# A fused attention and MoE kernel: input fetched earlier, batches interleaved, activation table loaded ahead, token sums as an extra matmul column

## The chip, the cores and the metric

The kernel runs on one core of a Trainium2 chip. The metric is the device time of one execution in microseconds (us). It includes about 2 us around the span that the profile shows, from the first to the last instruction: the profiled run of the kernel before took 255.27 us and its span is 253.5 us. PE is TensorE, PEld its weight loads, DVE is VectorE, ACT ScalarE, POOL GpSimd, SP SyncE.

## The reference

Eight batches go through a small cross attention between 512 tokens and 32 state rows for each of 8 heads, in both directions. Its result, 544 rows a batch, goes through a two-layer network with SiLU.

```python
scores = scale * x @ state.T            # (B,H,512,32)
a  = softmax(scores);   xread = a @ state       # 512 rows of 64 per head
a2 = softmax(scores.T); sread = a2 @ x          # 32 rows of 64 per head
x_moe = concat([xread, sread]) -> (8*544, 512)
out = silu(x_moe @ w_in) @ w_out                # d_ff = 2048
```

The kernel folds the state into the first weight: `W1 = state_blockdiag @ w_in`, so that `G1 = silu(W1.T @ aT)` needs only the normalised attention weights `aT`, and `G2 = G1.T @ w_out`. The sread rows are few and are done for all batches at the end (called batch 8).

## The kernel before

A batch passes through these steps, and each name is a helper that the schedule calls. The kernel keeps eight PSUM banks (the buffers that matmuls write), named o0, o1, w0, w1, h0, h1, a0 and a1; in the cuts below AB and HB stand for the pairs a0/a1 and h0/h1, and DA and DD for the two engines that copy a pair out (VectorE and ScalarE, or VectorE twice). aT is the normalised attention weights, transposed.

```python
def g1(b, ft):     # 2 matmuls of 512 columns, then SiLU on ScalarE
    ...
    nc.scalar.activation(g[b % 2][:, ft, :], bk[:], func=SILU, bias=0.0)
def g2(b, tt, ft, bk): ...      # 1 matmul of 512 columns, accumulated over 16 ft
def w1_m / w1_e                 # W1 = state x w_in, 8 small matmuls; copies out of PSUM
def cast_x, x_T, sc, ex         # x to bf16, transposes, scores, exponentials (EXP table)
def norm_s, norm_m, a_T         # row sums and reciprocal, multiply, transposes of the weights
def sread_m(b, bk):
    v = bank[bk]
    for half in range(2):
        for c in range(4):
            for kt in range(KT):
                nc.tensor.matmul(v[ds(32 * kt, 32), ds(D * half, D)],
                    en[b % 2][:, c, half, kt, :], x_n[b % 2][:, kt, c, half, :], ...)
    for half in range(2):               # the sums over tokens: a column of ones
        for c in range(4):
            nc.tensor.matmul(v[:, ds(128 + half, 1)],
                en[b % 2][:, c, half, :, :], ones[:], ...)
```

The schedule is written by hand. All weights are requested first, in chunks of 512 KB on the POOL queue; x of batch 1 is requested in the middle of batch 0. From batch 2 on it runs in phases: phase k does the G2 of batch k and, woven into it, the attention and G1 of batch k+1.

```python
load_w(0); load_st(1)
for j in range(1, 4): load_w(j)
...
sread_t(0, "a1", "dve")
W1x(0, 1, AB, DA)
gate(1)                      # makes the load of x wait until here
load_x(1, nc.sync)
cast_x(1, "dve", (0, 1)); cast_x(1, "pool", (2, 3))
...
for k in range(2, 7):
    n = k + 1
    ex(n, 0, 2, "a0"); ex(n, 2, 2, "a1")          # loads the EXP table
    W1p(n, 0); norm_s(n); norm_m(n, "pool")
    add(fill, 18, W1p(n, 1), sread_m(n, "a1"), sread_n(n, "a1"))
    add(fill, 29, a_T(n, (("a0", "act"),)))
    for i in range(16):
        add(fill, 32 + 1.9 * i, g1(n, i))          # the first one loads the SiLU table
    phase(k, fill)                                 # 64 G2, with the fill between them
```

The softmax here doesn't subtract the row's maximum and nothing guards it: scores larger than these inputs give would overflow.

## Time and profile before

| | kernel before |
|---|---|
| median | 256.44 us (3 runs, 254.75 to 257.2) |
| span, mean granted clock | 253.5 us, 0.980 |
| PE / ACT / DVE / POOL busy | 90% / 50% / 38% / 17% |

The first view is the windows view of the kernel before: for each stretch of time its length and each engine's busy time, with the number of instructions. PEclk is the granted clock of TensorE as a share of full speed; the last two columns are the DMA engines' busy share (in this view it exceeds 1 at times) and what they moved.

```profile
...
core 0: us, PE busy (x) PEld busy (x) DVE busy (x) ACT busy (x) POOL busy (x), PEclk, DMA share, GB/s
12.08:14.48 2.40, 1.81 (x17) 0.99 (x18) 1.17 (x3) 1.19 (x2) 1.05 (x2) 0.50 1.33 199
14.48:31.00 16.52, 15.97 (x111) 6.08 (x111) 2.02 (x7) 7.66 (x14) 3.17 (x5) 0.88 1.23 219
31.00:34.50 3.50, 0.00 (x0) 0.00 (x0) 0.95 (x3) 0.38 (x1) 0.98 (x3) 1.00 0.96 118
34.50:54.80 20.30, 16.72 (x127) 7.71 (x127) 9.12 (x18) 9.85 (x15) 2.53 (x3) 0.92 0.18 56
...
118.50:144.80 26.30, 24.89 (x218) 12.02 (x218) 11.60 (x22) 14.16 (x23) 4.74 (x9) 1.00 0.26 80
...
```

From 118.5 us on PE is busy for 24.89 of 26.3 us: these phases are bound by TensorE. Before 54.8 us it is different: from 14.48 us PE is busy for 15.97 of 16.52 us, but at a mean clock of 0.88; in the third row it does nothing at all for 3.5 us, and in the fourth it is busy for 16.72 of 20.3 us.

The second view is the timeline of PE in the kernel before. Columns: start, duration, engine, source line, operation, out<-in and the number of instructions merged; in brackets the idle time before and what ended it.

```profile
...
12.08 1.03 PE L181 MATMUL ps_a<-ident,an 128*128 128x128 bf16 x8 [1.66 <-DVE an L165]
...
14.48 2.74 PE L255 MATMUL ps_h<-aT,W 128*128 128x512 bf16 x6 [0.59 <-DVE W L79]
...
18.72 0.42 PE L191 MATMUL ps_a<-x_n,en 128*32 128x64 bf16 x32
19.07 0.35 PE L202 MATMUL ps_a<-ones,en 128*128 128x1 bf16 x8
19.29 0.59 PE L255 MATMUL ps_h<-aT,W 128*128 128x512 bf16 x2
...
29.66 1.03 PE L255 MATMUL ps_h<-aT,W 128*128 128x512 bf16 x4
34.52 0.40 PE L128 MATMUL ps_a<-ident,x_n 128*128 128x128 bf16 x4 [3.83 <-DVE x_n L79]
...
42.16 0.90 PE L234 MATMUL ps_a<-w_in_sb,sbd 64*32 64x512 bf16 x8 [1.73 <-ACT en L150]
...
```

The line of 34.52 us shows the hole: the transposes of x of batch 1 wait for DVE's cast, which waits for the DMA. The lines of 18.72 and 19.07 us show the sread group: 32 matmuls of 64 columns take 0.35 us from start to start of the next, and the eight matmuls of one column after them take 0.22 us.

The third view is the timeline of all engines in phase 3, around its first G1.

```profile
...
127.37 1.02 ACT L83 ACTIVATE aT<-ps_a 128x1024 bf16<-128x1024 bf16 x1 [6.44 <-PE ps_a L181]
...
128.44 0.59 PE L255 MATMUL ps_h<-aT,W 128*128 128x512 bf16 x2 [0.47 <-ACT aT L83]
...
129.12 1.28 ACT L263 ACT_TABLE_LOAD   x1 [0.72 <-PE ps_h L255]
...
129.52 0.59 PE L279 MATMUL ps_o<-w_out_sb,g 128*128 128x512 bf16 x2
...
130.41 1.09 ACT L263 ACTIVATE g<-ps_h 128x512 bf16<-128x512 f32 x2
131.06 0.59 PE L255 MATMUL ps_h<-aT,W 128*128 128x512 bf16 x2 [0.94 <-ACT g L263]
...
```

The first G1 waits for the copy of aT on ACT (128.44 us). Then ACT loads the SiLU table (129.12 us, 1.28 us) before it can drain that G1, and the third G1 has no free bank until 131.06 us.

### The profile page before, as it was taken

The numbers are of one execution on the slowest core, as the hardware profiler recorded it, in microseconds if no ns is written. First come the engines' busy times: TensorE is split into PE (matmuls) and PEld (weight loads), VectorE is DVE, ScalarE is ACT, GpSimd is POOL, SyncE is SP. The second block draws the span as 40 slices with busy tenths as digits, with TensorE's granted clock in tenths as the row PEclk, the third lists the DMA queues.
The fourth block names the chain that finished last, engine by engine and source line by source line (L and its number), as shares of the span: only waits on it lengthen the run. The fifth ranks groups of instructions, "written<-read, shape, count | busy, mean of one in ns | idle before, by whom it ended". The sixth has DMA issues, their size and how long they took to land.

```text
span 253.5 us, 4473 instructions
## 1 busy us (share of the span) xinstructions
PE 226.9 (90%) x1832; PEld 112.4 (44%) x1832; DVE 95.8 (38%) x187; ACT 126.4 (50%) x201; POOL 43.8 (17%) x81
## 2 busy tenths in 40 slices
PE   5699846899978999799979997999799988999994
PEld 4534223335334544354435443544354444466653
DVE  3722032482671447132914192409330850011110
ACT  3644516456816670757075726563466437733300
POOL 4732020322070005200340034002400110000000
PEclk9959989999999999999999999999999999999999
DMA  6999930086001116110810081017201120111112
GB/s 178 169 202 206 251 39 0 0 276 224 4 36 47 44 49 202 43 41 21 230 41 30 14 243 51 0 44 208 86 0 41 44 83 3 41 43 41 59 68 84
DMA packets 19829, 22.08 MB, mean 87 GB/s; under 512 B 3040, under 2 KB 15584, under 8 KB 19808
## 3 DMA queue, kind: packets, MB, share of 16 engines
q1 hardware_dynamic: 12576, 16.39, 19.8%
q0 software_dynamic: 6128, 4.42, 11.7%
q10 hardware_dynamic: 1104, 0.98, 1.1%
q8 instruction: 14, 0.23, 0.3%
q14 instruction: 7, 0.06, 0.1%
HBM read 17.30 MB, written 8.91 MB: 103 GB/s over the span
## 4 chain that ended last, share of the span: by engine, by line
PE 77%; ACT 7%; DVE 6%; DMA 6%; issue 3%; ACTq 0%; DVEq 0%
PE ps_o L279 39%; PE ps_h L255 21%; DMA x_f<-in_x_dram 6%; PE ps_h L266 3%; PE ps_a L128 3%; ACT aT L83 2%; PE ps_w L279 2%; PE ps_w L234 2%; ACT g L263 2%; PE ps_a L181 2%; DVE W L79 2%; DVE rs L160 2%; PE ps_a L139 1%; ACT L263 1%; DVE x_n L79 1%
## 5 line engine op out<-in xcount | busy, mean ns | idle before, releaser
L279 PE MATMUL ps_o<-w_out_sb,g 128*128 128x512 bf16 x480 | 133.4, 381 | 1.1 <-DVE o_sb L79 1.0
L263 ACT ACTIVATE g<-ps_h 128x512 bf16<-128x512 f32 x128 | 75.4, 597 | 48.0 <-PE ps_h L255 47.2
L255 PE MATMUL ps_h<-aT,W 128*128 128x512 bf16 x256 | 76.8, 385 | 9.5 <-ACT g L263 4.7
L279 PEld LDWEIGHTS <-g 128*128 128x128 bf16 x512 | 47.8, 98 | 53.6 <-issue 6.6
L79 DVE COPY o_sb<-ps_o 128x512 f32<-128x512 f32 x30 | 20.3, 684 | 65.4 <-PE ps_o L279 65.4
L255 PEld LDWEIGHTS <-W 128*128 128x128 bf16 x256 | 24.8, 99 | 40.2 <-issue 12.9
L165 POOL TENSOR_TENSOR an<-en,rs 128x1024 bf16<-128x1024 bf16 x7 | 13.4, 1913 | 124.0 <-DVE rs L161 112.3
L83 ACT ACTIVATE aT<-ps_a 128x1024 bf16<-128x1024 bf16 (+1 forms) x8 | 7.3, 918 | 37.8 <-PE ps_a L181 37.8
L81 POOL CAST x_n<-x_f 128x256 bf16<-128x256 f32 x52 | 18.5, 405 | 22.4 <-DMA x_f<-in_x_dram 22.4
L79 DVE CAST W<-ps_w 128x512 bf16<-128x512 f32 x29 | 18.7, 684 | 7.8 <-PE ps_w L234 7.8
L128 PEld LDWEIGHTS <-x_n 128*128 128x128 bf16 x128 | 9.2, 106 | 8.5 <-DVE x_n L79 5.8
L79 DVE CAST W<-ps_h 128x512 bf16<-128x512 f32 x20 | 12.8, 681 | 0.0
L160 DVE TENSOR_REDUCE rs<-en 128x32 f32<-128x1024 bf16 (+1 forms) x11 | 10.2, 923 | 6.9 <-ACT en L150 6.9
L128 PE MATMUL ps_a<-ident,x_n 128*128 128x128 bf16 x112 | 8.9, 225 | 4.2 <-DVE x_n L79 4.2
L79 DVE COPY sbd<-ps_a 64x128 bf16<-64x128 bf16 x14 | 4.0, 288 | 21.9 <-PE ps_a L117 21.8
L79 DVE COPY xT<-ps_a 128x1024 bf16<-128x1024 bf16 x13 | 8.9, 691 | 8.8 <-PE ps_a L128 4.9
L274 ACT ACTIVATE g_s<-ps_h 128x256 bf16<-128x256 f32 x16 | 6.2, 384 | 11.6 <-PE ps_h L266 11.6
L263 ACT ACT_TABLE_LOAD x7 | 9.0, 1283 | 3.7 <-PE ps_h L255 3.6
L279 PE MATMUL ps_w<-w_out_sb,g 128*128 128x512 bf16 x32 | 10.3, 406 | 0.0
L266 PE MATMUL ps_h<-xsT,w_in_sb 128*128 128x256 bf16 x64 | 9.6, 273 | 0.0
L79 DVE CAST x_n<-x_f 128x256 bf16<-128x256 f32 x12 | 3.9, 383 | 13.9 <-DMA x_f<-in_x_dram 13.9
L150 ACT ACT_TABLE_LOAD x7 | 9.0, 1283 | 0.1
(60 smaller groups left out, 139.8 us busy)
## 6 DMA issues: line engine op xcount, KB each, us to landing
out_dram<-o_sb SPq DMA_DIRECT2D x32, 256.0 KB, 2.4
x_f<-in_x_dram SPq DMA_DIRECT2D x7, 1024.0 KB, 6.7
w_in_sb<-in_moe_w_in_dram POOLq DMA_DIRECT2D x4, 512.0 KB, 11.6
w_out_sb<-in_moe_w_out_dram POOLq DMA_DIRECT2D x4, 512.0 KB, 13.9
x_f<-in_x_dram SPq DMA_DIRECT2D x2, 256.0 KB, 3.0
x_f<-in_x_dram ACTq DMA_DIRECT2D x2, 256.0 KB, 3.8
out_dram<-o_sb ACTq DMA_DIRECT2D x1, 256.0 KB, 2.5
st_nat<-in_state_dram POOLq DMA_DIRECT2D x7, 32.0 KB, 14.2
```

Of the source, the lines that this page charges most:

```text
L79: nc.vector.tensor_copy(dst, src)
L81: nc.gpsimd.tensor_copy(dst, src)
L83: nc.scalar.activation(dst, src, func=COPY, bias=0.0)
L128: nc.tensor.transpose(v[:, kt % 2, c, :], x_n[b % 2][:, kt, c, :, :], ident[:])
L150: nc.scalar.activation(en[b % 2][:, :, :, ds(kt, n), :].rearrange("p c h k s -> p k (c h) s"), v[:, ds(kt % 2, n)], func=EXP, bias=0.0, sc ...
L160: nc.vector.tensor_reduce(v, en[b % 2][:, :, :, ds(kt, n), :], axis=AX, op=ADD)
L165: e.tensor_tensor(an[b % 2][:, :, :, ds(kt, n), :].rearrange("p c h k s -> p (c h) k s"), en[b % 2][:, :, :, ds(kt, n), :].rearrange("p c ...
L255: nc.tensor.matmul(bk[:], W1[b % 2][:, half, ds(128 * ft, 128)], aT[b % 2][:, half, :, :], start=(half == 0), stop=(half == 1), skip_group ...
L263: nc.scalar.activation(g[b % 2][:, ft, :], bk[:], func=SILU, bias=0.0)
L266: nc.tensor.matmul(bk[:, 0:256], w_in_sb[:, kt, ds(128 * ft, 128)], xsT[:, kt, :, :, :], start=(kt == 0), stop=(kt == KT - 1), skip_group_ ...
L274: nc.scalar.activation(g_s[:, ft, :], bk[:, 0:256], func=SILU, bias=0.0)
L279: nc.tensor.matmul(bank[bk][:, c0:c1], src[:, ft, ds(128 * tt, 128)], w_out_sb[:, ft, c0:c1], start=(ft == 0), stop=(ft == 15), skip_group ...
```

## The change

The change has three intents: to fill the hole at the start by fetching x of batch 1 right behind the first weight chunks and by interleaving G1 of batch 1 with batch 0; to take small matmuls away from PE; and to take two waits out of each phase. Its core, with cuts marked:

```diff
-    ones = pers.tile([128, 1], BF16, name="ones")
-    x_n = [pers.tile([128, KT, 4, 2, D], BF16, ...
+    x_n = [pers.tile([128, KT, 4, 132], BF16, ...      # columns 1 and 130 hold ones
 ...  sread_m: 65 columns instead of 64, the group with ones[:] removed
-                        v[ds(32 * kt, 32), ds(D * half, D)],
+                        v[ds(32 * kt, 32), ds((D + 1) * half, D + 1)],
-                        x_n[b % 2][:, kt, c, half, :],
+                        x_n[b % 2][:, kt, c, ds(1 + (D + 1) * half, D + 1)],
 ...  start
-        load_w(0)
+        load_wi(0); load_wo(0)
         load_st(1)
-        for j in range(1, 4):
-            load_w(j)
+        load_x(1, nc.gpsimd, 0, 2)
+        load_x(1, nc.gpsimd, 2, 2)
 ...  the other weights follow later; W1 of batch 0 before its a_T; normalisation in
 ...  halves instead of quarters, shared with POOL
+        for ft in range(4):
+            g1(0, ft)
+        G2(0, 0) ... G2(0, 3), between them cast_x(1), xTs(1), scs(1)
+        exs(1); norm_s(1); norm_m(1, "dve")
+        W1x(0, 1, AB, DA)
+        W1x(1, 0, HB, DA)
+        nc.scalar.preload_act_table(SILU)
+        a_T(1, (("a0", "dve"),))
+        g1(0, 4) ... g1(0, 7), G2(0, 4), g1(1, 0), G2(0, 5), g1(1, 1), ...   # to g1(1, 10)
 ...  phases
-                w1_e(b, 2 * i + j, WP[j], ("dve", "dve"))
+                w1_e(b, 2 * i + j, WP[j], DD if j == 0 else ("act", "act"))
+            add(fill, s, L(nc.scalar.preload_act_table, SILU))     # after the exponentials and the first W1 copies
-            add(fill, 29, L(a_T, n, (("a0", "act"),)))
+            add(fill, a0, L(a_T, b, (("a0", "act"),)))             # a0 = 24
-                add(fill, 32 + 1.9 * i, L(g1, n, i))
+                add(fill, sg + dg * i, L(g1, b, i))                # 28 + 2.15 * i
```

Batch 1 becomes a phase of the same form, with its last five G1 at the start.

More of the change, by code (lines that the diff above doesn't have):

```diff
@@ L47 @@
     x_f = [pers.tile([128, KT, 2, 256], FP32, name=f"x_f{i}") for i in range(2)]
-    x_n = [pers.tile([128, KT, 4, 2, D], BF16, name=f"x_n{i}") for i in range(2)]
+    x_n = [pers.tile([128, KT, 4, 132], BF16, name=f"x_n{i}") for i in range(2)]
     xT = [pers.tile([128, KT, 4, 128], BF16, name=f"xT{i}") for i in range(2)]
@@ L94, in gate, with load_wi @@
         nc.vector.memset(x_f[b % 2][ds(0, 1), 0, 0, ds(0, 1)], 0.0)
-    def load_w(j):
+    def load_wi(j):
         nc.gpsimd.dma_start(
@@ L99, in load_w, with load_wo @@
         )
+    def load_wo(j):
         nc.gpsimd.dma_start(w_out_sb[:, ds(4 * j, 4), :], wout_re[:, ds(4 * j, 4), :])
@@ L110, in cast_x @@
                     eng,
-                    x_n[b % 2][:, kt, :, h, :],
+                    x_n[b % 2][:, kt, :, ds(2 + D * h, D)],
                     x_f[b % 2][:, kt, h, :].rearrange("p (c d) -> p c d", c=4),
@@ L128, in x_T @@
             nc.tensor.transpose(
-                v[:, kt % 2, c, :], x_n[b % 2][:, kt, c, :, :], ident[:]
+                v[:, kt % 2, c, :], x_n[b % 2][:, kt, c, ds(2, 128)], ident[:]
             )
@@ L199, in sread_m @@
                     )
-        for half in range(2):
-            for c in range(4):
-                nc.tensor.matmul(
-                    v[:, ds(128 + half, 1)],
-                    en[b % 2][:, c, half, :, :],
-                    ones[:],
-                    start=(c == 0),
-                    stop=(c == 3),
-                    skip_group_check=True,
-                )
     def sread_n(b, bk):
         v = bank[bk]
-        nc.vector.reciprocal(srec[:], v[:, 128:130])
+        nc.vector.reciprocal(srec[:], v[:, 0:130:129])
         nc.vector.tensor_tensor(
             sr[:],
-            v[:, 0:128].rearrange("p (h d) -> p h d", h=2),
+            v[:, 1:129].rearrange("p (h d) -> p h d", h=2),
             srec[:].unsqueeze(2).to_broadcast([128, 2, D]),
@@ L311 @@
         nc.scalar.dma_start(st0_f[:], state[0].rearrange("h ns d -> ns h d"))
-        load_x(0, nc.sync, 0, 1)
-        load_x(0, nc.scalar, 1, 1)
-        load_x(0, nc.sync, 2, 1)
-        load_x(0, nc.scalar, 3, 1)
+        for kt in range(KT):
+            load_x(0, nc.sync, kt, 1)
         nc.vector.memset(zeros[:], 0.0)
         nc.vector.memset(sbd[:], 0.0)
-        nc.vector.memset(ones[:], 1.0)
+        for i in range(2):
+            nc.vector.memset(x_n[i][:, :, :, 1:131:129], 1.0)
         make_identity(nc, ident[:])
@@ L321 @@
         cp("pool", st_nat[:, 0, :], st0_f[:])
-        load_w(0)
+        load_wi(0)
+        load_wo(0)
         load_st(1)
-        for j in range(1, 4):
-            load_w(j)
-        for b in range(2, B):
-            load_st(b)
-        warm(18, "o0")
+        load_x(1, nc.gpsimd, 0, 2)
+        load_x(1, nc.gpsimd, 2, 2)
+        warm(20, "o0")
         XB = ("o0", "o1", "w0", "w1")
         SB = ("h0", "h1", "a0", "a1")
-        st_T(0, "a1", "act", "act")
-        warm(4, "h0")
-        cast_x(0, "dve", (0, 1, 2, 3))
-        for i in range(5):
-            if i < 4:
-                x_T(0, i, XB[i])
-                x_Te(0, i, 1, XB[i], "act")
-            if i > 0:
-                sc(0, i - 1, SB[i - 1])
-                if i == 1:
-                    warm(4, "a1")
-                ex(0, i - 1, 1, SB[i - 1])
-                norm_s(0, i - 1, 1)
-                norm_m(0, "dve", i - 1, 1)
-        nc.scalar.preload_act_table(SILU)
-        warm(14, "o0")
-        a_T(0, (("a0", "dve"), ("a1", "act")))
-        w1_m(0, 0, ("w0", "w1"))
-        w1_e(0, 0, ("w0", "w1"), ("dve", "act"))
-        st_T(1, "a0", "dve", "dve")
-        OB = ("o0", "o1", "w0", "w1")
         AB = ("a0", "a1")
+        HB = ("h0", "h1")
+        OB = XB
+        DA = ("dve", "act")
+        DD = ("dve", "dve")
         def G2(b, ft):
@@ L364, in W1x, with exs @@
             w1_e(b, j, bks, engs)
-        def exps(b):
+        def exs(b):
             ex(b, 0, 2, "a0")
             ex(b, 2, 2, "a1")
-            norm_s(b)
-            norm_m(b, "pool")
         def xTs(b, q, eng):
@@ L379, in scs @@
                 sc(b, kt, AB[q])
-        DA = ("dve", "act")
-        g1(0, 0)
-        g1(0, 1)
-        g1(0, 2)
+        cast_x(0, "dve", (0,))
+        x_T(0, 0, XB[0])
+        x_Te(0, 0, 1, XB[0], "act")
+        cast_x(0, "dve", (1,))
+        st_T(0, "a1", "act", "dve")
+        cast_x(0, "dve", (2, 3))
+        for kt in range(KT):
+            if kt < 3:
+                x_T(0, kt + 1, XB[kt + 1])
+                x_Te(0, kt + 1, 1, XB[kt + 1], ("act", "act", "dve")[kt])
+            sc(0, kt, SB[kt])
+            ex(0, kt, 1, SB[kt])
+            if kt == 1:
+                warm(6, "o0")
@@ L386 @@
+        norm_s(0, 0, 2)
+        norm_m(0, "pool", 0, 2)
+        norm_s(0, 2, 2)
+        norm_m(0, "dve", 3, 1)
+        norm_m(0, "pool", 2, 1)
+        nc.scalar.preload_act_table(SILU)
+        warm(10, "o0")
+        w1_m(0, 0, ("w0", "w1"))
+        w1_e(0, 0, ("w0", "w1"), ("act", "act"))
+        a_T(0, (("a0", "dve"), ("a1", "dve")))
+        load_wi(1)
+        load_wo(1)
+        load_wi(2)
+        for ft in range(4):
+            g1(0, ft)
         G2(0, 0)
+        st_T(1, "a0", "dve", "dve")
@@ L387 @@
         sread_m(0, "a1")
         sread_n(0, "a1")
-        g1(0, 3)
         G2(0, 1)
         sread_t(0, "a1", "dve")
-        W1x(0, 1, AB, DA)
-        gate(1)
-        load_x(1, nc.sync)
-        cast_x(1, "dve", (0, 1))
-        cast_x(1, "pool", (2, 3))
-        G2(0, 2)
+        G2(0, 2)
+        cast_x(1, "dve", (0, 1, 2))
+        cast_x(1, "pool", (3,))
+        load_wo(2)
+        load_wi(3)
+        load_wo(3)
+        load_x(2, nc.gpsimd)
+        for b in range(2, B):
+            load_st(b)
@@ L398 @@
+        xTs(1, 0, "dve")
+        G2(0, 3)
+        xTs(1, 1, "act")
+        scs(1, 0)
+        scs(1, 1)
+        exs(1)
+        norm_s(1)
+        norm_m(1, "dve")
+        W1x(0, 1, AB, DA)
+        W1x(1, 0, HB, DA)
+        nc.scalar.preload_act_table(SILU)
+        a_T(1, (("a0", "dve"),))
         g1(0, 4)
-        G2(0, 3)
         g1(0, 5)
         g1(0, 6)
+        W1x(1, 1, AB, DA)
+        g1(0, 7)
         G2(0, 4)
-        g1(0, 7)
+        g1(1, 0)
         G2(0, 5)
-        W1x(0, 2, AB, ("act", "act"))
+        g1(1, 1)
@@ L407 @@
         G2(0, 6)
+        W1x(0, 2, AB, DA)
+        g1(1, 2)
+        G2(0, 7)
+        g1(1, 3)
         g1(0, 8)
-        G2(0, 7)
+        W1x(1, 2, AB, DA)
         g1(0, 9)
         g1(0, 10)
-        xTs(1, 0, "dve")
-        xTs(1, 1, "act")
+        g1(0, 11)
         G2(0, 8)
-        scs(1, 0)
-        scs(1, 1)
-        g1(0, 11)
-        exps(1)
+        g1(1, 4)
         G2(0, 9)
-        W1x(0, 3, AB, ("dve", "dve"))
+        g1(1, 5)
         G2(0, 10)
+        W1x(0, 3, AB, DA)
@@ L423 @@
+        g1(1, 6)
+        G2(0, 11)
+        g1(1, 7)
         g1(0, 12)
-        W1x(1, 0, AB, ("dve", "dve"))
-        G2(0, 11)
+        W1x(1, 3, AB, DA)
         g1(0, 13)
@@ L429, with W1p, phase @@
         G2(0, 12)
-        W1x(1, 1, AB, DA)
-        gate(2)
-        load_x(2, nc.sync)
-        load_x(3, nc.sync)
-        cast_x(2, "pool")
         g1(0, 15)
         G2(0, 13)
-        W1x(1, 2, AB, DA)
+        g1(1, 8)
         G2(0, 14)
-        a_T(1, (("a0", "dve"), ("a1", "act")))
-        st_T(2, "a0", "dve", "dve")
+        g1(1, 9)
         G2(0, 15)
-        g1(1, 0)
-        g1(1, 1)
+        g1(1, 10)
         for tt in range(4):
             o_e(0, tt, OB[tt], "dve")
-        W1x(1, 3, AB, ("dve", "dve"))
-        for ft in range(10):
-            g2(1, 0, ft, "o0")
-            g1(1, ft + 2)
-            if ft == 3:
-                xTs(2, 0, "dve")
-                xTs(2, 1, "dve")
-            if ft == 7:
-                scs(2, 0)
-                scs(2, 1)
-        ex(2, 0, 2, "a0")
-        ex(2, 2, 2, "a1")
-        g1(1, 12)
-        g1(1, 13)
-        g2(1, 0, 10, "o0")
-        W1x(2, 0, ("w0", "w1"), ("dve", "dve"))
-        g2(1, 0, 11, "o0")
-        for ft in range(12):
-            g2(1, 1, ft, "o1")
-            if ft == 3:
-                W1x(2, 1, ("w0", "w1"), ("dve", "dve"))
-                norm_s(2)
-                norm_m(2, "pool")
-                sread_m(1, "a1")
-            if ft == 8:
-                sread_n(1, "a1")
-                W1x(2, 2, ("w0", "w1"), ("dve", "dve"))
-            if ft == 11:
-                sread_t(1, "a1", "dve")
-        cast_x(3, "pool")
-        for ft in range(12, 16):
-            g2(1, 0, ft, "o0")
-            g2(1, 1, ft, "o1")
-            if ft < 14:
-                g1(1, ft + 2)
-            if ft == 13:
-                W1x(2, 3, ("w0", "w1"), ("dve", "dve"))
-        o_e(1, 0, "o0")
-        o_e(1, 1, "o1")
-        def phase(k, fill, tts=(0, 1, 2, 3)):
-            for tt in tts:
+        cast_x(2, "pool", (2, 3))
+        cast_x(2, "dve", (0, 1))
+        load_x(3, nc.sync)
+        WP = (("w0", "w1"), ("h0", "h1"))
+        def W1p(b, i):
+            for j in range(2):
+                w1_m(b, 2 * i + j, WP[j])
+            for j in range(2):
+                w1_e(b, 2 * i + j, WP[j], DD if j == 0 else ("act", "act"))
+        def phase(k, fill):
+            for tt in range(4):
                 bk = ("o0", "o1")[tt % 2]
@@ L501, in L @@
             return lambda: f(*a)
-        def att_tail(fill, b, s_m, s_t, s_a):
-            add(fill, s_m, L(sread_m, b, "a1"), L(sread_n, b, "a1"))
-            add(fill, s_t, L(sread_t, b, "a1", "dve"))
-            add(fill, s_a, L(a_T, b, (("a0", "dve"),)))
         def att_head(fill, b, s0, s1):
@@ L510, in att_head @@
             add(fill, s0 + 2, L(xTs, b, 0, "dve"))
-            add(fill, s0 + 4, L(xTs, b, 1, "dve"))
+            add(fill, s0 + 5, L(xTs, b, 1, "dve"))
             add(fill, s1, L(scs, b, 0))
             add(fill, s1 + 2, L(scs, b, 1))
-        fill = {}
-        add(fill, 34, L(a_T, 2, (("a0", "act"),)))
-        for i in range(16):
-            add(fill, 36 + 1.7 * i, L(g1, 2, i))
-        add(fill, 38, L(sread_m, 2, "a1"), L(sread_n, 2, "a1"))
-        add(fill, 42, L(sread_t, 2, "a1", "dve"))
@@ L521, with att_tail @@
-        att_head(fill, 3, 50, 58)
-        phase(1, fill, (2, 3))
-        WP = (("w0", "w1"), ("h0", "h1"))
-        def W1p(b, i):
-            for j in range(2):
-                w1_m(b, 2 * i + j, WP[j])
-            for j in range(2):
-                w1_e(b, 2 * i + j, WP[j], ("dve", "dve"))
+        def att_tail(fill, b, s, a0, sg, dg):
+            add(fill, s, L(exs, b), L(W1p, b, 0), L(norm_s, b), L(norm_m, b, "pool"))
+            add(fill, s, L(nc.scalar.preload_act_table, SILU))
+            add(fill, s + 14, L(W1p, b, 1), L(sread_m, b, "a1"), L(sread_n, b, "a1"))
+            add(fill, a0, L(a_T, b, (("a0", "act"),)))
+            add(fill, a0 + 2, L(sread_t, b, "a1", "dve"))
+            for i in range(16):
+                add(fill, sg + dg * i, L(g1, b, i))
@@ L533 @@
+        fill = {}
+        for i in range(11, 16):
+            add(fill, (i - 11) * 2, L(g1, 1, i))
+        add(fill, 6, L(sread_m, 1, "a1"), L(sread_n, 1, "a1"))
+        add(fill, 8, L(sread_t, 1, "a1", "dve"))
+        add(fill, 8, L(cast_x, 3, "pool"))
+        att_head(fill, 2, 9, 17)
+        att_tail(fill, 2, 20, 43, 46, 1.1)
+        att_head(fill, 3, 48, 58)
+        phase(1, fill)
         for k in range(2, 7):
-            n = k + 1
             fill = {}
-            ex(n, 0, 2, "a0")
@@ L537 @@
-            ex(n, 2, 2, "a1")
-            W1p(n, 0)
-            norm_s(n)
-            norm_m(n, "pool")
             if k + 2 < B:
                 load_x(k + 2, nc.sync)
-                cast_x(k + 2, "pool")
-            add(fill, 18, L(W1p, n, 1), L(sread_m, n, "a1"), L(sread_n, n, "a1"))
-            add(fill, 29, L(a_T, n, (("a0", "act"),)))
-            add(fill, 30, L(sread_t, n, "a1", "dve"))
-            for i in range(16):
-                add(fill, 32 + 1.9 * i, L(g1, n, i))
+            att_tail(fill, k + 1, 0, 24, 28, 2.15)
@@ L549 @@
             if k + 2 < B:
-                att_head(fill, k + 2, 40, 56)
+                add(fill, 0, L(cast_x, k + 2, "pool"))
+                att_head(fill, k + 2, 42, 56)
             phase(k, fill)
```

## The prediction

> **What bounds it.** One core, span 253.5 us. In phases 2 to 6 (one batch each) TensorE is the bound: the windows view gives PE 24.7 to 24.9 us busy of each 26.2 us phase at clock 1.00. Before 54.8 us it waits for data. The timeline shows two losses.
>
> 1. Prologue. Batch 0's attention transposes start at 12.08 us, the first G1 at 14.48 us, with granted clock 0.50; the first 512-column matmuls take 0.43 us each instead of 0.216. The Trainium skill ("TensorE: Matmul & The Clock Gate", Part 1) says that the array runs at half clock until about 3.4 us of activity; the trace agrees in the factor. Then x of batch 1 is fetched at 22.5 us behind all weights and lands at 33.5 us: PE idles from 31 to 34.5 us, and 1.7 us for the exponentials later. From 12.1 to 54.8 us I count about 27 us of PE work at full rate in 42.7 us.
> 2. Each phase 2 to 6: PE waits 0.47 us for the aT copy on ScalarE and 0.94 us because the SiLU table load (1.28 us) sits between the first two G1 (waits view: 3.1 us in 6 and 4.7 us in 5).
>
> **What the change does, costed.**
> - Token sums as a 65th column remove 64 one-column matmuls. Eight take 0.22 us of PE's issue; 32 of 64 columns take 0.35 us. "TensorEngine Tiling (Array Packing)", Instruction Overhead, says that a one-column matmul costs as much as 60 columns; the trace has 27 ns each. Widening is free: -0.2 us a batch.
> - SiLU table loaded right after the exponentials: -0.9 us a phase. a_T at step 24 instead of 29, one more matmul before G1: -0.2 to -0.5 us. W1 copies shared by VectorE and ScalarE bring the normalisation about 1 us earlier, which the earlier a_T needs; slack 0.5 us. Phases become about 24.8 us: five save 7 to 7.5 us.
> - Start: fewer, larger normalisations, W1 before a_T, first G1 near 12 us.
> - x of batch 1 behind the first two weight chunks (landed by 13.4 us) should land near 17 us, scores be done at 21.5 us. But the chain EXP load 1.3, exponentials 1.1, reduce and reciprocal 1.5, multiply about 1.2, W1 copies 0.7 each is now bare on PE: banks a0/a1 are held until the exponentials are done. I expect PE nearly idle from 21.5 to 27.5 us: longer than the old stall, with cold matmuls after it.
> - After it no weight is late, and G1 of batch 1 fills ScalarE-bound places. Left in batch 0's stage: 23 G1 (9.9), 48 G2 (10.4), W1 (1.4) = 21.7 us, plus 4 to 5 us of ScalarE pacing and cold clock: batch 1's G2 start at 54 us with eleven G1 done (before: 54.8 us with two). Phase 1 is 28 us of work plus 1: phase 2 starts at 83 us instead of 92.4. Saved: about 9.5 us.
>
> **Time.** -9.5 - 7.2 gives 239.7 us; last phase and tail are unchanged. Prediction 239.7, range 235 to 246. Faster by over 2%: 0.95; within: 0.04; slower: 0.01.
>
> **What would show it.** Single-column group gone, sread matmuls as short as before; no PE wait of 0.9 us on ScalarE's g; phases of 24.6 to 25.0 us; x of batch 1 landing at 16 to 18 us; the PE hole near 21 to 28 us; phase 2 starting at 81 to 85 us.
>
> **What would make it wrong.** x of batch 1 landing much later; a longer cold stretch after the stall; normalisation late for a_T at step 24, a new stall in each phase; odd alignment of 65-column slices slowing matmuls or casts.

## The result

The changed kernel takes 240.22 us (median of 4 runs, 239.66 to 240.24), the kernel before 255.99 us (median of 4 runs, three of them those of the table above). The ratio is 0.938 (95% interval 0.933 to 0.943). Ratios here and below are the mean time of one kernel's runs over that of the other's in the same rounds, so not quite the ratio of the medians. Every "ratio" is to the kernel before; 0.001 of it is 0.255 us.

Timeline of PE in the changed kernel, the start (same columns as above):

```profile
...
11.35 0.63 PE L225 MATMUL ps_w<-w_in_sb,sbd 64*32 64x512 bf16 x8 [0.72 <-DMA w_in_sb<-in_moe_w_in_dram]
...
13.14 3.14 PE L246 MATMUL ps_h<-aT,W 128*128 128x512 bf16 x8
...
17.13 0.43 PE L192 MATMUL ps_a<-x_n,en 128*32 128x65 bf16 x32
17.50 0.60 PE L270 MATMUL ps_o<-w_out_sb,g 128*128 128x512 bf16 x2
...
23.33 0.41 PE L140 MATMUL ps_a<-sbd,xT 128*128 128x64 bf16 x8 [0.88 <-ACT xT L82]
25.23 1.11 PE L225 MATMUL ps_a<-w_in_sb,sbd 64*32 64x512 bf16 x8 [1.50 <-ACT en L151]
...
29.22 1.01 PE L182 MATMUL ps_a<-ident,an 128*128 128x128 bf16 x8 [2.45 <-DVE W L78]
30.03 2.69 PE L246 MATMUL ps_h<-aT,W 128*128 128x512 bf16 x6
...
32.99 0.60 PE L246 MATMUL ps_h<-aT,W 128*128 128x512 bf16 x2
...
```

The old hole is gone, and there is a new one near the place where the prediction put it: PE waits 0.88, 1.50 and 2.45 us, for the copy of x's transposes, for the exponentials and for the W1 copy that frees bank a0. The six matmuls at 30.03 us take 0.43 us each, at half clock. The sread group at 17.13 us still takes 0.37 us to the next start, and no group of single columns follows it.

The windows view of the changed kernel over that hole:

```profile
...
24.00:28.00 4.00, 1.42 (x16) 0.23 (x15) 2.23 (x3) 3.21 (x6) 0.72 (x2) 0.71 1.24 206
28.00:32.00 4.00, 2.78 (x13) 1.61 (x14) 2.46 (x4) 1.44 (x3) 1.40 (x2) 0.50 1.21 251
...
```

The granted clock falls to 0.71 and 0.50; from 32 to 36 us it is 0.94 on the mean, and 1.00 after that. The timeline below is of phase 3 of the changed kernel, all engines:

```profile
...
112.29 1.28 ACT L478 ACT_TABLE_LOAD   x1
...
113.17 1.91 POOL L166 TENSOR_TENSOR an<-en,rs 128x1024 bf16<-128x1024 bf16 x1 [18.97 <-DVE rs L162]
...
115.77 0.61 PE L182 MATMUL ps_a<-ident,an 128*128 128x128 bf16 x8
...
116.47 1.02 ACT L82 ACTIVATE aT<-ps_a 128x1024 bf16<-128x1024 bf16 x1 [1.80 <-PE ps_a L182]
...
116.70 0.59 PE L270 MATMUL ps_o<-w_out_sb,g 128*128 128x512 bf16 x2
...
117.55 0.59 PE L246 MATMUL ps_h<-aT,W 128*128 128x512 bf16 x2 [0.25 <-ACT aT L82]
...
```

The SiLU table is loaded at 112.29 us, five microseconds ahead of the first G1; the waits at 129 to 131 us of the kernel before have no counterpart. A wait for aT is left: PE's previous matmuls were issued at 116.70 and 116.92 us, and the next one would have started at 117.13 us; it starts at 117.55 us. The phases are marked by their first W1 matmul into the h banks. That of phase 2 in the kernel before (timeline of PE):

```profile
...
92.23 0.56 PE L234 MATMUL ps_h<-w_in_sb,sbd 64*32 64x512 bf16 x8
...
```

and in the changed kernel:

```profile
...
84.38 0.56 PE L225 MATMUL ps_h<-w_in_sb,sbd 64*32 64x512 bf16 x8
...
```

With the later ones, the distances are:

| | phase 2 starts | then each phase takes |
|---|---|---|
| before | 92.23 us | 26.4, 26.24, 26.24, 26.24 us |
| changed | 84.38 us | 24.84, 24.74, 24.73, 24.74 us |

So 7.85 us came off before phase 2 and about 1.5 us off each phase from 2 on.

### The profile page after: what moved, and what is told of

Its sections match the earlier page's. It is cut to its first block, busy times and chain, and to the rows that moved or that the text cites. A ratio compares the mean times of both kernels' runs of the same rounds, so it can differ in the third digit from the quotient of the medians.

```text
span 237.9 us, 4311 instructions
## 1 busy us (share of the span) xinstructions
PE 222.2 (93%) x1764; PEld 111.2 (47%) x1764; DVE 83.8 (35%) x162; ACT 138.3 (58%) x224; POOL 43.9 (18%) x79
## 4 chain that ended last, share of the span: by engine, by line
PE 85%; ACT 5%; DMA 4%; DVE 3%; issue 1%; POOL 0%; ACTq 0%
PE ps_o L270 44%; PE ps_h L246 24%; PE ps_w L270 3%; DMA w_in_sb<-in_moe_w_in_dram 3%; PE ps_h L257 3%; PE ps_a L129 3%; ACT aT L82 3%; PE ps_w L225 2%; PE ps_a L182 2%; DMA st_f<-in_state_dram 1%; PE ps_a L192 1%; PE ps_a L140 1%; PE ps_h L225 1%; ACT g L254 1%; PE ps_a L225 1%
## 5 line engine op out<-in xcount | busy, mean ns | idle before, releaser
L270 PE MATMUL ps_o<-w_out_sb,g 128*128 128x512 bf16 x480 | 131.2, 379 | 0.0
L166 POOL TENSOR_TENSOR an<-en,rs 128x1024 bf16<-128x1024 bf16 (+2 forms) x8 | 13.3, 1665 | 96.2 <-DVE rs L162 96.2
L80 POOL CAST x_n<-x_f 128x256 bf16<-128x256 f32 x46 | 16.2, 400 | 39.9 <-PE ps_a L140 26.3
L78 DVE CAST W<-ps_w 128x512 bf16<-128x512 f32 x24 | 15.4, 683 | 1.8 <-PE ps_w L225 1.6
L82 ACT ACTIVATE W<-ps_h 128x512 bf16<-128x512 f32 x25 | 13.7, 603 | 0.5 <-PE ps_h L225 0.5
L82 ACT ACTIVATE aT<-ps_a 128x1024 bf16<-128x1024 bf16 x6 | 6.1, 1023 | 10.4 <-PE ps_a L182 10.4
L151 ACT ACT_TABLE_LOAD x7 | 9.0, 1283 | 3.2 <-PE ps_a L140 3.1
L270 PE MATMUL ps_w<-w_out_sb,g 128*128 128x512 bf16 x32 | 9.5, 379 | 0.0
L78 DVE CAST W<-ps_a 128x512 bf16<-128x512 f32 x6 | 4.1, 690 | 14.7 <-PE ps_a L225 14.7
L151 ACT ACTIVATE en<-ps_a 128x512 bf16<-128x512 f32 (+1 forms) x16 | 8.4, 568 | 1.0 <-PE ps_a L140 0.9
## 6 DMA issues: line engine op xcount, KB each, us to landing
x_f<-in_x_dram POOLq DMA_DIRECT2D x1, 1024.0 KB, 15.6
```

The costliest lines, as they stand in the source:

```text
L78: nc.vector.tensor_copy(dst, src)
L80: nc.gpsimd.tensor_copy(dst, src)
L82: nc.scalar.activation(dst, src, func=COPY, bias=0.0)
L151: nc.scalar.activation(en[b % 2][:, :, :, ds(kt, n), :].rearrange("p c h k s -> p k (c h) s"), v[:, ds(kt % 2, n)], func=EXP, bias=0.0, sc ...
L166: e.tensor_tensor(an[b % 2][:, :, :, ds(kt, n), :].rearrange("p c h k s -> p (c h) k s"), en[b % 2][:, :, :, ds(kt, n), :].rearrange("p c ...
L270: nc.tensor.matmul(bank[bk][:, c0:c1], src[:, ft, ds(128 * tt, 128)], w_out_sb[:, ft, c0:c1], start=(ft == 0), stop=(ft == 15), skip_group ...
```

## The experiments

Kernels of one group ran on the same chip beside the kernel before. Where I compare two kernels of different groups, I use their ratios to the kernel before.

### First group: the small parts, one at a time

**b_sum**: the kernel before, with only the token sums as a 65th column (the first two hunks of the diff above).

> The kernel before with only the token sums moved into a 65th column. Theory: PE is full in the phases, so the 8 groups of one-column matmuls (0.22 us each) come off directly: 1.5 to 1.8 us less than before (ratio 0.993 to 0.994), PE busy down by about 2 us, the 32 matmuls of 65 columns still 0.35 to 0.37 us apart. Rival: the one-column group hides behind weight loads or other waits, or the odd alignment eats it: ratio 0.998 to 1.002.

Measured: 253.77 us, ratio 0.9949 (0.9923 to 0.9974), so 0.7 to 2.0 us less, 1.3 in the middle. After the first, the phases of its trace take 26.05 us instead of 26.24. Those 0.19 us are the 0.22 us of the removed group less what the wider slices cost: the 32 matmuls of 65 columns take 0.36 to 0.37 us to the next start, against 0.35 us with 64. The group came off almost in full because PE is full.

**b_silu**: the kernel before, with only the table load moved.

```diff
             ex(n, 2, 2, "a1")
+            nc.scalar.preload_act_table(SILU)
             W1p(n, 0)
```

> The kernel before with only the SiLU table loaded right after the exponentials in phases 2 to 6. Theory: the 0.94 us wait of PE on g disappears in 5 phases, phase period 26.24 to 25.3 us, 4.5 us less in all (ratio 0.982). Rival: the wait is mostly ScalarE's pace at the start of G1 and comes back as ScalarE pacing a few matmuls on: under 2 us less (ratio above 0.992).

Measured: 249.45 us, ratio 0.9768 (0.9743 to 0.9793): 5.9 us less, more than expected. The waits view of the kernel before and of this one, for PE (in total, times, longest):

```profile
...
PE ps_h L255 <- ACT g L263: 4.7, 5, 0.9
PE ps_a L128 <- DVE x_n L79: 4.2, 2, 3.8
PE ps_h L255 <- ACT aT L83: 3.1, 6, 0.7
...
```

```profile
...
PE ps_a L128 <- DVE x_n L79: 5.4, 2, 5.3
PE ps_h L255 <- ACT aT L83: 3.4, 6, 0.7
...
```

The wait for g is gone from the phases, and the wait for aT is about as it was. Its phases take 25.30, 25.14, 25.42 and 25.14 us where the kernel before has 26.4, 26.24, 26.24 and 26.24: 1.1 us in most of them, so about 5.2 us in five. The rest of the 5.9 us is not the edit's by this trace: phase 2 already starts at 90.96 us instead of 92.23, and before it the two kernels are the same, so the start differs from run to run by such amounts. The waits view had said 0.94 us a phase. The difference from 1.1 us is how a wait is measured: the timeline above has the last two G2 at 129.52 us, issued 0.216 us apart, so the next could start at 129.95 us; it started at 131.06 us, which is 1.11 us later. The profile counts as idle only the time after the modelled end of the last matmul, and in a full stream that end lies after the start of the next one. The Trainium skill ("Perfetto Trace Analysis", Identifying the Most-Contended Engine) warns that the busy share of matmuls is a poor measure of the distance to the roofline, because they are pipelined. This shows a fault of the same kind in idle time: a matmul modelled at 0.38 us (lines of one matmul) outlasts the 0.216 us to the next start, so a wait comes out 0.17 us too short.

**a_nosilu**: the changed kernel without the early table load in its phases (that one line removed).

> The changed kernel without the early SiLU table load in its phases (the load then happens at the first G1). Theory: the wait comes back in phases 1 to 6, +0.7 to 0.95 us each, 4 to 5.5 us more than the changed kernel (ratio to before about 0.957 instead of 0.938). Rival as above: under 2 us.

Measured: 244.25 us, ratio 0.9568 (0.9535 to 0.9601), where 0.957 was expected. The wait is back in each of its six phases:

```profile
...
PE ps_h L246 <- ACT g L254: 3.8, 6, 0.7
...
```

**a_w1dve**: the changed kernel with the W1 copies of the phases all on VectorE again.

```diff
-                w1_e(b, 2 * i + j, WP[j], DD if j == 0 else ("act", "act"))
+                w1_e(b, 2 * i + j, WP[j], DD)
```

> The changed kernel with all W1 copies of the phases on VectorE. Theory: the normalisation chain ends about 1.3 us later, which is more than the 0.5 us of slack at a_T in step 24: PE waits 0.5 to 0.9 us on the normalised weights in each of 6 phases, 3 to 5 us more than the changed kernel. Rival: VectorE is only a third busy and the slack covers it: within 0.5 us of the changed kernel.

Measured: 240.76 us, ratio 0.9412 (0.9371 to 0.9453). The interval includes both ratios of the changed kernel (0.9379, and 0.9407 in after_again below), and its phases take 24.84, 24.74 and 24.73 us, as with the shared copies. The theory fell. In its trace the multiply on POOL starts at 115.84 us, and PE comes to a_T at 117.95 us:

```profile
...
115.84 1.91 POOL L166 TENSOR_TENSOR an<-en,rs 128x1024 bf16<-128x1024 bf16 x1 [18.79 <-DVE rs L162]
...
```

```profile
...
117.95 0.61 PE L182 MATMUL ps_a<-ident,an 128*128 128x128 bf16 x8
...
```

The multiply ends at 117.75 us, 0.20 us before it is needed. In the changed kernel (lines of 113.17 and 115.77 us above) it ends 0.69 us before. So sharing the copies buys 0.5 us of slack that nothing uses, and the earlier a_T did not need it. It buys 0.5 and not 1.3 us because DVE, freed of two copies, then waits 0.62 us for the exponentials.

### Second group: the start

**b_xearly**: the kernel before, with only x of batch 1 moved forward in the queue. Its casts stay where they were.

```diff
         load_st(1)
+        load_x(1, nc.gpsimd, 0, 2)
+        load_x(1, nc.gpsimd, 2, 2)
 ...
-        gate(1)
-        load_x(1, nc.sync)
```

> The kernel before with only x of batch 1 moved to the place right behind the first weight chunks on the same queue; everything else in its order. Theory: the PE hole from 31 to 34.5 us closes with its cold matmuls, and the later weight chunks cost at most 1 us: 3.5 to 4.5 us less (ratio 0.983 to 0.986). Rival: the wait only moves to the weight chunks, which come 3.9 us later: 0 to 1 us less (ratio above 0.996).

Measured: 249.95 us, ratio 0.9782 (0.9733 to 0.9831): 5.6 us less, 4.3 to 6.8 by the interval. In its trace PE waits for no weight chunk, and phase 2 starts at 87.09 us instead of 92.23:

```profile
...
87.09 0.56 PE L234 MATMUL ps_h<-w_in_sb,sbd 64*32 64x512 bf16 x8
...
```

About 0.7 of these 5.1 us were there before PE used x of batch 1 (W1 of chunk 1 at 20.00 us instead of 20.73), so the trace leaves some 4.4 us for the early x itself, which is within what was expected. The wait did not move to the weights, which the kernel before had fetched earlier than it needed them. This is as large a part of the gain before phase 2 as any, and it is two lines.

**a_xlate**: the changed kernel, with x of batch 1 requested behind all weights.

> The changed kernel with x of batch 1 fetched behind all weights. Theory: its order of work needs x early; PE stops after its third G2 (about 19 us) until x lands near 33 us and then has the bare chain: 12 to 14 us more than the changed kernel, ratio to before 0.985 to 0.995. Rival (the gain is in the order of G1 and G2, and the fetch matters little): under 4 us more.

Measured: 254.68 us, ratio 0.9982 (0.9944 to 1.002). The whole gain is lost, though the phases of its trace still take 24.7 us. Phase 2 of its trace starts at 99.09 us, 14.7 us later than in the changed kernel, and one wait does it:

```profile
...
PE ps_a L129 <- DVE x_n L78: 14.9, 1, 14.9
...
```

The new order places the transposes of batch 1 ahead of most of batch 0, so it depends on the early fetch more than the old order did.

**a_nog1**: the changed kernel, with G1 0 to 10 of batch 1 taken out of batch 0's stage and put at the start of phase 1.

```diff
-        g1(1, 0)     # and so on to g1(1, 10), each at its place
 ...
+        g1(1, 0)
+        g1(1, 1)
+        for i in range(2, 16):
+            add(fill, i - 2, L(g1, 1, i))
```

> The changed kernel with the first eleven G1 of batch 1 taken out of batch 0's stage and done at the start of phase 1. The same PE work. Theory: G1 bursts without G2 of other work are paced by ScalarE (0.6 us each against 0.43 us), so 2 to 4 us more than the changed kernel. Rival: the weights are all there and PE is full either way: within 0.7 us.

Measured: 241.74 us, ratio 0.9473 (0.9411 to 0.9535), which is 1.7 to 2.4 us above the changed kernel's ratios of 0.9379 and 0.9407, with intervals that overlap. The trace puts about half of that down to the edit. From G1 number 7 of batch 0 to the first W1 of phase 1 it takes 31.89 us (34.14 to 66.03 us). The changed kernel takes 30.82 us and a_w1dve, with the same code there, 30.81 us. So the interleaving gives 1.1 us. The rest came before: this run waited 1.71 us for the first weight chunk, the changed kernel's profiled run 0.72 us. The expected 2 to 4 us were too many.

**a_fill**: the changed kernel, with the new hole filled by work that needs neither a0/a1 nor the EXP table.

```diff
         scs(1, 0)
+        W1x(0, 1, HB, DD)
         scs(1, 1)
         exs(1)
+        nc.scalar.preload_act_table(SILU)
         norm_s(1)
         norm_m(1, "dve")
-        W1x(0, 1, AB, DA)
-        W1x(1, 0, HB, DA)
-        nc.scalar.preload_act_table(SILU)
-        a_T(1, (("a0", "dve"),))
         g1(0, 4)
         g1(0, 5)
+        W1x(1, 0, AB, DD)
         g1(0, 6)
+        a_T(1, (("a0", "dve"),))
+        g1(0, 7)
         W1x(1, 1, AB, DA)
-        g1(0, 7)
```

> The changed kernel with the hole near 24 to 30 us filled: W1 of chunk 1 in banks h0/h1 ahead of the exponentials, the first G1 of that chunk ahead of batch 1's transposes. Theory: the hole is a chain over PSUM banks a0/a1 and ScalarE's tables and not a wait for weights (chunk 1 landed before 21.7 us): 2.5 to 4 us less than the changed kernel, ratio to before 0.922 to 0.928. Rival: the next weight chunk holds it instead: under 1 us less.

Measured: 238.25 us, but spread from 236.71 to 240.01, ratio 0.9341 (0.9281 to 0.94): 1.0 to 1.7 us less than the changed kernel's two ratios, with intervals that overlap. By the trace the stretch from the first G1 to phase 1 took 48.2 us (12.69 to 60.89) instead of 50.7 (13.14 to 63.81); the profiled run is the fastest of the four. It is a smaller gain than expected, and neither theory had it: no weight was late, but G1 now waits 1.50 us for ACT behind the SiLU load, and a_T 1.2 us for DVE's copy out of bank a0.

### Third group: the hole again, and the sum of the parts

**after_again**: the changed kernel, unaltered.

> The changed kernel once more, to stand on the same chip beside the next three: ratio to before 0.938 to 0.941. Its first wait for weights differs from run to run (0 to 1.9 us in the traces so far), so its times should spread over about 2 us.

Measured: 239.93 us (239.68 to 241.0), ratio 0.9407 (0.938 to 0.9435). In its trace the first chunk was late by 1.3 us, against 0.7 us in the first profiled run, and yet phase 2 starts at 84.33 us where it started at 84.38 us then. The times spread over 1.3 us, not 2.

**a_warm**: dummy matmuls in the hole, in banks that are free at that moment.

```diff
+        warm(14, "h0")
         W1x(0, 1, AB, DA)
         W1x(1, 0, HB, DA)
         nc.scalar.preload_act_table(SILU)
+        warm(18, "a1")
         a_T(1, (("a0", "dve"),))
```

> The changed kernel with 14 and 18 dummy matmuls in the hole between 24 and 30 us, in banks that are free there. Theory: the six matmuls after the hole take 0.43 us each only because the array has gone to half clock; kept warm they take 0.216 us, and 0.7 to 1.5 us come off; granted clock 1.00 from 28 to 36 us. Rival: ScalarE's 0.6 us a tile paces G1 there anyway: within 0.4 us.

Measured: 239.41 us, ratio 0.9375 (0.9351 to 0.9399), 0.8 us below after_again, with intervals that overlap a little. The windows view of a_warm, for the stretch that had clock 0.50:

```profile
...
24.00:28.00 4.00, 2.38 (x42) 1.62 (x43) 1.32 (x2) 3.43 (x6) 0.77 (x2) 1.00 1.25 208
28.00:32.00 4.00, 2.54 (x29) 1.76 (x28) 3.37 (x5) 2.13 (x4) 1.40 (x2) 1.00 1.21 248
...
```

The clock stays at 1.00. From W1 of chunk 1 to the first W1 of phase 1 the trace takes 37.5 us (26.18 to 63.72) where after_again takes 38.6 (25.18 to 63.76). The difference lies between a_T and G1 number 7 of batch 0: 2.75 us (30.16 to 32.91) instead of 3.78 (29.17 to 32.95). It is not that a late start is made up later: a_w1dve, with the changed kernel's code there, came to W1 of chunk 1 at 27.01 us and took 38.9 us to phase 1. So the half clock after the hole costs about 1 us, and ScalarE does not pace it all away. The times alone would not settle it.

**b_three**: b_sum, b_silu and b_xearly together.

> The kernel before with the three separable parts together: x of batch 1 early, the sums as a column, the SiLU table early in the phases. If they add up: 5.3 + 1.3 + 5.5 = 12 us less than before, ratio 0.952 to 0.956, which leaves 3.5 to 4 us of the change's 16 for the new order (G1 of batch 1 between the chunks, the shorter start, a_T earlier). Rival: they overlap (the same PE time counted twice): ratio above 0.96.

Measured: 243.24 us, ratio 0.951 (0.948 to 0.954): 12.5 us less. The three parts alone gave 1.3, 5.9 and 5.6 us, 12.8 in sum. They add up. The changed kernel in the same group is 0.0103 lower, which is 2.6 us. That is all that the new order of batches 0 and 1, the new start, the shared copies and the earlier a_T bring together. By the traces over half of it is the phases: 25.06 us on the mean in b_three (four phases from 84.76 to 185.0 us), 24.76 us in the changed kernel, 0.3 us in each of five. This fits the wait for aT, which the waits views put at 3.4 us in 6 in b_three and 1.6 us in 6 in the changed kernel; the earlier a_T was not run alone. Up to phase 2 the traces differ by only 0.4 us (84.76 against 84.33 and 84.38 us).

**a_best**: a_fill's idea carried further, and the wait for aT.

```diff
+        cast_x(1, "dve", (0, 1)); cast_x(1, "pool", (3,))
         sread_t(0, "a1", "dve")
         G2(0, 2)
-        cast_x(1, "dve", (0, 1, 2)); cast_x(1, "pool", (3,))
+        cast_x(1, "dve", (2,))
 ...     as a_fill to norm_m(1, "dve"), then:
+        g1(0, 4); g1(0, 5)
+        W1x(1, 0, AB, DD)
+        g1(0, 6); G2(0, 4); g1(0, 7); G2(0, 5)
+        a_T(1, (("a0", "dve"),))
+        W1x(1, 1, AB, DA)
+        g1(1, 0); g1(1, 1); G2(0, 6)
 ...
-            att_tail(fill, k + 1, 0, 24, 28, 2.15)
+            att_tail(fill, k + 1, 0, 24, 30, 2.05)
```

> The changed kernel with the hole filled (W1 of chunk 1 before the exponentials, first G1 and G2 of the chunk before batch 1's transposes, casts of x ahead of the sread transpose's copy) and G1 of the phases starting at step 30 instead of 28. Theory: 3 to 4.5 us less from the hole, 0.2 us a phase from the aT wait: 4 to 5 us less than the changed kernel, ratio to before 0.920 to 0.925. Rival: the weights or ScalarE's pace take it back: under 1.5 us.

Measured: 233.13 us (232.51 to 235.46), ratio 0.9148 (0.9111 to 0.9186). That is 6.6 us below after_again, more than expected, and the fastest version. The waits of PE in its waits view with the longest single wait:

```profile
...
PE ps_h L246 <- ACT g L254: 1.9, 2, 1.5
...
PE ps_w L225 <- DMA w_in_sb<-in_moe_w_in_dram: 1.1, 1, 1.1
...
```

The wait for aT is down to 0.4 us once, in batch 1's phase (1.6 us in 6 before). What is left is the SiLU load after the exponentials of batch 1 and the first weight chunk. The phases take 24.49, 24.32, 24.32 and 24.33 us, 0.42 us less than in the changed kernel in most of them. That is the aT wait as measured between starts (117.13 to 117.55 us above), not the 0.25 us in its bracket. Phase 2 starts at 82.20 us instead of 84.33. Together the trace shows 4.1 us: span 233.7 against 237.8 us. The profiled run happens to be the slowest of the six, 235.46 us; the other five took 232.51 to 234.71 us. For the faster ones there is no trace, so 2 to 3 us of this version's gain are not explained here. One hint: the mean granted clock was 0.993 in the profiled run and 0.997 to 1.000 in the other five, so a shorter half-clock stretch may be part of it; that is not shown.

## Why the prediction was right

The prediction said 239.7 us, and 240.22 us were measured. The parts:

| step | predicted | measured |
|---|---|---|
| sums as a column | 0.2 us a batch | 0.19 us a phase; 1.3 us in all (b_sum) |
| SiLU table early | 0.9 us a phase | 1.1 us a phase (b_silu), 5.9 us in all |
| phases | 24.8 us | 24.73 to 24.84 us |
| x of batch 1 in hand | 16 to 18 us | 17.22 us: POOL's first cast of it starts |
| first G1 | near 12 us | 13.14 us, 13.51 us |
| scores of batch 1 done | 21.5 us | 23.6 us: the second group starts at 23.33 us |
| hole | 21.5 to 27.5 us | waits from 22.5 to 29.2 us; G1 goes on at 30.03 us |
| batch 1's G2 start | 54 us | 54.38 us |
| phase 2 starts | 83 us | 84.4 us |

**Right, and shown.** The bound in the phases, the removal of the single columns, the table load, the early x and the new hole are as told. b_sum, b_silu, a_nosilu and b_xearly each show one of these alone.

**Right in sum, with errors that partly cancel.** The start was placed 1 us too early and the end of the hole 2.5 us too early. First, the W1 matmuls at the start wait for the first weight chunk (0.7 us at 11.35 us in the trace). Second, x of batch 1 had landed at 17.22 us, but DVE cast its first quarter only at 18.93 us, because in its program order the copy of sread's transpose comes first (timeline of all engines in the changed kernel):

```profile
...
17.22 0.74 POOL L80 CAST x_n<-x_f 128x256 bf16<-128x256 f32 x2 [3.02 <-DMA x_f<-in_x_dram]
...
18.93 2.41 DVE L78 CAST x_n<-x_f 128x256 bf16<-128x256 f32 x6
...
```

Third, the copy of x's transposes on ACT, 0.88 us of PE's time, was not in the sum. Against that, the 4 to 5 us of ScalarE pacing and cold clock were too many: from G1 number 4 to batch 1's G2 it took 24.35 us (30.03 to 54.38), and the prediction had allowed 26.5 us for it. Then phase 1 took 30.0 us (54.38 to 84.38) where 29 were allowed.

That the total came within 0.5 us is in part luck. The start saved 7.85 us by the traces and not 9.5. The phases and the tail saved 7.75 us (15.6 us between the spans, less 7.85) and not 7.2. And the prediction started from the median of 256.44 us, where the fourth run made it 255.99.

**Wrong.** "W1 copies shared by VectorE and ScalarE bring the normalisation about 1 us earlier, which the earlier a_T needs". a_w1dve shows that it comes 0.5 us earlier and is not needed. Also mis-sized was the wait for g: 0.94 us from the idle column, 1.11 us between starts.

**What the total does not tell.** I put 9.5 us down to the early x with the new order, without dividing them. b_three and a_xlate divide them: the early fetch gives 5.6 us in the old order, and the new order adds little while it makes the early fetch indispensable. a_nog1 gives its interleaving 1.1 us; a_best shows that the hole which it left was worth at least 2 us more (phase 2 at 82.20 instead of 84.33 us). The shorter start (fewer, larger normalisations, W1 before a_T) was not run alone, and neither was the earlier a_T.

Of the prediction's citations of the Trainium skill, "TensorEngine Tiling (Array Packing)", Instruction Overhead, says that a matmul of one column costs as much as one of 60. The case agrees that one column is not nearly free: 27 ns each (0.22 us for eight). It does not test the equality, because the 64-column matmuls here each use a 32-column strip of the array (tile_position in sread_m) and come every 11 ns (0.35 us for 32). What mattered was that removing 64 of the narrow ones took 1.3 us off, and widening 256 others by a column cost 0.02 us in each group of 32. "TensorE: Matmul & The Clock Gate", Part 1, says half clock after an idle window of about 3.4 us; the trace has 0.50 and 0.43 us a matmul after the hole, and a_warm has 1.00. No single wait of that length was needed: the clock was at 0.50 from 25.75 us on, when PE's longest wait in the hole had been 1.50 us.

## What to carry to other kernels

Measure a wait on a full TensorE from start to start of its matmuls, not by the idle time in the bracket: here 0.94 us was 1.11, and 0.25 us was 0.42. When several engines take part in one chain, first ask what its resources are (here two PSUM banks, an activation table and one engine's program order), and move other work into the hole by giving it other banks, as a_best does. Before a large reordering, try its small parts alone: here 12.5 of about 15 us lay in three small edits.

## What the Trainium skill lacked or had wrong

- "ScalarE: Activation LUTs", What ACT_TABLE_LOAD costs, gives 1283 ns for the load and 1380 ns of drain, 2.66 us a switch. The load is 1.283 us on the mean here, too, but no drain of that size shows on either side of it: in the kernel before the exponentials end at 66.45 us, the load runs from 66.47 to 67.75 us, and the SiLU starts at 67.76 us. A switch took 1.3 us.
- No page that I read tells how much the first weight chunk's landing can vary: PE waited 0 to 1.9 us for it in the traces of the changed kernel and its variants, which request it in the same way.
- "Perfetto Trace Analysis" warns of the busy time of pipelined matmuls and that their end is estimated, but does not draw from it that the idle time before a matmul comes out too short: by 0.17 us a wait here.
